# Splitting the transpose of a pair's last row tile in an attention and MoE kernel

## The chip, the cores and the metric

The kernel runs on one core of a Trainium2 chip. The metric is the device time of one execution in microseconds (us); lower is better. The engines are named as in the profile: PE is TensorE, DVE is VectorE, ACT is ScalarE, POOL is GpSimd, and SP is SyncE, which here only issues DMAs.

## What is computed

Attention with a learned position bias, and behind it a feed-forward layer with two weight matrices:

```
B, H, S, D = 4, 8, 576, 64
scores = q @ k.T / sqrt(D) + bias        # bias[h,i,j] from log1p(|i-j|) / log1p(i) through a small MLP
attn   = exp(scores - max) / (sum + 1e-9)
x      = (attn @ v), reshaped to [B*S, H*D] = [2304, 512]
h      = x @ w_in                        # 512 -> 2048
g      = h * clip(h + 3, 0, 6) / 6
out    = g @ w_out                       # 2048 -> 512
```

## The kernel before, in words

**Units.** Two heads make a pair; a batch has four pairs. The 576 query rows of a batch are cut in two parts: part 0 has rows 0 to 255, part 1 rows 256 to 575 (320 rows). A unit is one batch, one pair, one part. All 16 units of part 0 come first, then the 16 units of part 1, batch by batch. The change touches the units of part 1 alone.

**Tiles.** A unit of part 1 has five row tiles of 128 rows (`ORDER`, numbers 4 to 8): rows 256 to 383 of the first head and of the second, rows 384 to 511 of the first and of the second, and a last tile (number 8) with the 64 remaining rows 512 to 575 of both heads, the first head's in partitions 0 to 63 and the second head's in 64 to 127. The tiles of all units stand in one list, and `front(n)` issues work for several of them at once: the maximum of tile n, the scores of tile n+1, the normalization of tile n-1 (`hl`, high part by ACT, L129), the low part of tile n-2 (DVE, L146), the transpose of tile n-3 (`soft_turn`, L648), the product with V of the unit whose last tile is n-5 (`pv_step`, L719) and the low part of x (`x_low`) of the unit whose last tile is n-6. `back(n)` issues `x_high` (ACT, L733) of the unit whose last tile is n-5, and the exponential of tile n (L583).

**Transposes.** The attention rows `hl` are 128 x 1152 in fp16: the high part in columns 0 to 575 and the low part in 576 to 1151. A DMA transpose on SP's queue turns one tile into a 128 x 9 x 128 piece of `at`, at the column `COLS[t]`. In a unit of part 1 `at` has 640 columns, the first head's 320 tokens in columns 0 to 319 and the second head's in 320 to 639.

**x.** The product with V, `pv_ps`, lies in one PSUM bank: the first head in partitions 0 to 63 and the second in 64 to 127, with the columns in the order of `at`. Since the last tile is transposed as one piece to columns 256 to 383, the second head's tokens begin with their last 64. `XPARTS` puts them right: ACT writes the high part of x with three instructions (64 rows x 320, x 64 and x 256 columns), and DVE the low part with three more of the same shapes. The profile calls both L146 (DVE) and L733 (ACT), with `x` as output.

**Banks.** From the stretch that matters here on, `pv_ps` shares four PSUM banks (`w_bank`) with the feed-forward layer's `h_ps` (L794) and `o_ps` (L817). Banks are taken in turn, so the fourth bank taken after a `pv_ps` is that same bank, and PE waits there until DVE's x has read it. The scores `s_ps` (L560) take two other tiles of PSUM in turn, free when DVE's L572 has read them. An `h_ps` bank is free when DVE's L777 (`t`) has read it.

**Order.** PE's instructions keep the order of the program from tile 37 on, and SP's from tile 45 on. DVE, ACT and POOL are ordered by the framework's scheduler.

Of the kernel before, what the change touches and what calls it, by code (L numbers as in the profile page):

```python
# [14 lines left out]
AF = mybir.ActivationFunctionType  # L15
# [20 lines left out]
def attention_moe_kernel(  # L36
# [17 lines left out]
    nc = tc.nc  # L54
# [61 lines left out]
    pscale = {}  # L116
# [28 lines left out]
    def low_part(out, full, scale, high):  # L145
        nc.vector.scalar_tensor_tensor(  # L146
            out=out, in0=full, scalar=scale, in1=high, op0=ALU.mult, op1=ALU.subtract
        )
# [249 lines left out]
    QW = (256, 320)  # L398
# [106 lines left out]
        return out, src  # L505

    ORDER = [(0, 0), (0, 1), (1, 0), (1, 1), (2, 0), (2, 1), (3, 0), (3, 1), (4, 0)]
    COLS = [0, 256, 128, 384, 0, 384, 128, 512, 256]
    UT = (range(4), range(4, 9))
    units = [(b, p, u) for u in range(2) for b in range(B) for p in range(PAIRS)]  # L510
    tiles = [(0, p, t) for ts in ((0, 1), (2, 3)) for p in range(2) for t in ts]
# [10 lines left out]
    a_t = {}  # L522
    at_t = {}
# [87 lines left out]
    def direct(b, p, t):  # L611
        return b < cfg["fb"] and t < 4

    def unit_tile(n):
        b, p, t = tiles[n]
        u = int(t >= 4)
        if (b, p, u) not in at_t:
            if direct(b, p, t):
                at = at_p.tile([128, 5, 512], F32, tag=f"at{p % 2}", name="atf")
            else:  # L620
                at = at_p.tile([128, 9, 2 * QW[u]], F16, tag=f"at{p % 2}", name="at")
            at_t[b, p, u] = at
        return at_t[b, p, u][:, :, COLS[t]:COLS[t] + 128]

    def soft_low(n):
        if direct(*tiles[n]):
            bt, sm = a_t.pop(n)
            tp = s_bank("t_ps").rearrange("p a b -> p (a b)")
            for c in range(5):
                j = 128 * c if c < 4 else 448  # L630
                nc.tensor.transpose(tp[:, 128 * c:128 * c + 128], bt[:, j:j + 128], eye_sb)  # L631
            src = tp[:, 0:640].rearrange("p (c i) -> p c i", c=5)
            if pick("tv", n) == "A":
                nc.scalar.activation(out=unit_tile(n), in_=src, func=AF.Copy)  # L634
            else:
                nc.vector.tensor_copy(out=unit_tile(n), in_=src)
            return
        bt, sm, hl = a_t[n]
        r = sm[:, 3:4]
        if hl_mode(n) in "RS":  # L640
            nc.gpsimd.tensor_sub(out=hl[:, S:], in0=bt, in1=hl[:, 0:S])
        else:
            low_part(hl[:, S:], bt, r, hl[:, 0:S])
        a_t[n] = hl

    def soft_turn(n):
        if not direct(*tiles[n]):
            nc.sync.dma_start_transpose(out=unit_tile(n), in_=a_t.pop(n))  # L648

    XPARTS = [  # L650
        [(slice(0, 128), 0, 256, 0)],
        [
            (slice(0, 64), 0, 320, 0),
            (slice(64, 128), 0, 64, 256),
            (slice(64, 128), 64, 320, 0),
        ],
    ]

    def x_tile(b, u):
        if (b, u) not in x_t:  # L660
            x_t[b, u] = x_p.tile([128, 2, KC, QW[u]], F16, tag="x", name="x")
        return x_t[b, u]
# [27 lines left out]
    def x_first(b, p):  # L690
        ps = pv_t.pop((b, p, 0))
        n = 256
        x = x_tile(b, 0)
        xr = hl_p.tile([128, 2, n], F32, tag="hl", name="xr")
        xs, rb = xr[:, 0], xr[:, 1]
        nc.scalar.activation(
            out=rb, in_=ps[:, 1, 0:n], func=AF.Copy,
            scale=pscale["x1"][:, p:p + 1] if b else pscale["v0"][1],
        )
        if cfg["xp"]:  # L700
            nc.scalar.activation(out=xs, in_=ps[:, 0, 0:n], func=AF.Copy)
            nc.gpsimd.tensor_mul(out=xs, in0=xs, in1=rb)
        else:
            nc.vector.tensor_mul(out=xs, in0=ps[:, 0, 0:n], in1=rb)
        xh = x[:, 0, p]
        nc.scalar.activation(out=xh, in_=xs, func=AF.Copy)
        nc.gpsimd.tensor_sub(out=x[:, 1, p], in0=xs, in1=xh)
# [19 lines left out]
    def x_high(b, p, u):  # L727
        if direct(b, p, 4 * u):
            return x_first(b, p)
        ps = pv_t[b, p, u]  # L730
        x = x_tile(b, u)
        for rows, lo, hi, tok in XPARTS[u]:
            nc.scalar.activation(  # L733
                out=x[rows, 0, p, tok:tok + hi - lo], in_=ps[rows, lo:hi], func=AF.Copy,
                scale=pscale["x"][rows, p:p + 1],
            )

    def x_low(b, p, u):
        if direct(b, p, 4 * u):
            return  # L740
        ps = pv_t.pop((b, p, u))
        x = x_tile(b, u)
        for rows, lo, hi, tok in XPARTS[u]:
            low_part(
                x[rows, 1, p, tok:tok + hi - lo], ps[rows, lo:hi],
                pscale["x"][rows, p:p + 1], x[rows, 0, p, tok:tok + hi - lo],
            )

    def ffn(b, u):
        x = x_t.pop((b, u))  # L750
# [235 lines left out]
    def front(n):  # L986
# [13 lines left out]
        if unit_at(n - 6):  # L1000
            x_low(*unit_at(n - 6))
# [8 lines left out]
        if at(n - 3):  # L1010
            soft_turn(n - 3)
# [12 lines left out]
    def back(n):  # L1024
        if unit_at(n - 5):
            x_high(*unit_at(n - 5))
        if at(n):
            soft_exp(n)
# [60 lines left out]
    for cs in (slice(512, LT), slice(0, 512)):  # L1089
        nc.vector.tensor_scalar(  # L1090
            out=T[:, cs], in0=T[:, cs], scalar1=w1_sb, scalar2=None, op0=ALU.mult
# [13 lines left out]
    for c, pat in enumerate(pats):  # L1105
        for k in range(4):
            if pat[k]:
                rows = slice(32 * k, 32 * k + 32)
# [111 lines left out]
    for n in range(-1, NT + 7):  # L1220
# [19 lines left out]
        if done is not None and done != (0, 0):  # L1240
            b, u = done
# [76 lines left out]
```

## Time and profile before

| what | value |
|---|---|
| time before, median of 3 runs (lowest, highest) | 681.77 us (680.17, 683.64) |
| the profiled execution's own time | 680.92 us |
| its span, from the first to the last instruction | 679.1 us |
| PE busy | 631.2 us, 93% of the span |
| ACT busy | 519.8 us, 77% |
| DVE busy | 478.9 us, 71% |
| POOL busy | 210.6 us, 31% |
| mean granted PE clock | 0.987 of full speed |

Busy shares are averages over the whole span. Most of PE's idle time lies in the first 240 us, in which the weights and the bias tables are prepared; the units of part 1 are worked on from about 340 to 610 us. The profiled execution's time and its span differ by 1.8 us, which lie before the first and after the last instruction.

### The profile page before, as it was taken

How to read it: one execution, taken by the hardware profiler on the slowest of the kernel's cores; microseconds unless marked ns; L12 is line 12 of the kernel's file. 1: busy time of each engine (PE TensorE's matmuls, PEld its weight loads, DVE VectorE, ACT ScalarE, POOL GpSimd, SP SyncE). 2: the span in 40 equal slices, each digit the busy share in tenths (PEclk: the TensorE clock that was granted, in tenths of full speed). 3: DMA queues.
4: the chain of work that ended last, by engine and by line, in shares of the span. 5: the costliest groups of instructions: out<-in, count | busy, mean ns of one | idle time of the engine just before them, and what ended most of it. 6: DMA issues, size and time to landing. Idle time of an engine off the chain costs nothing. (4 is left out here: it accounts for less than half of the span.)

```text
span 679.1 us, 14803 instructions
## 1 busy us (share of the span) xinstructions
PE 631.2 (93%) x5424; PEld 449.8 (66%) x5424; DVE 478.9 (71%) x1150; ACT 519.8 (77%) x1032; POOL 210.6 (31%) x267
## 2 busy tenths in 40 slices
PE   7677889787998999999999999999999999999997
PEld 2224546555676767688887786767776777777775
DVE  7889977999737887777688777777777768811310
ACT  7986877887939997998699878987799779922620
POOL 1111115855102441154134413541244313310420
PEclk9997999997999999999999999999999999999999
DMA  8899768571768979979999899979977796420000
GB/s 295 297 339 339 296 246 317 184 271 57 192 182 208 236 191 283 217 217 203 280 278 232 175 202 195 190 148 181 206 178 150 166 197 126 98 60 20 1 11 29
DMA packets 176136, 130.56 MB, mean 192 GB/s; under 512 B 137792, under 2 KB 145216, under 8 KB 175040
## 3 DMA queue, kind: packets, MB, share of 16 engines
q1 hardware_dynamic: 166272, 114.14, 67.5%
q10 hardware_dynamic: 9792, 15.49, 7.1%
q8 instruction: 42, 0.69, 0.4%
q14 instruction: 30, 0.25, 0.1%
HBM read 77.54 MB, written 15.49 MB: 137 GB/s over the span
## 5 line engine op out<-in xcount | busy, mean ns | idle before, releaser
L794 PE MATMUL h_ps<-x,wi 128*128 128x256 f16 (+1 forms) x1536 | 199.7, 287 | 8.3 <-DVE t L777 4.0
L817 PE MATMUL o_ps<-g,wo 128*128 128x256 f16 (+1 forms) x1536 | 195.8, 286 | 0.3 <-DVE t L777 0.3
L794 PEld LDWEIGHTS <-wi 128*128 128x128 f16 x1536 | 147.2, 98 | 56.5 <-issue 14.4
L817 PEld LDWEIGHTS <-wo 128*128 128x128 f16 x1536 | 147.0, 98 | 47.0 <-issue 10.0
L773 POOL TENSOR_TENSOR g<-t,g 128x256 f16<-128x256 f32 (+1 forms) x128 | 101.6, 805 | 165.1 <-ACT g L771 155.4
L583 ACT ACTIVATE bt<-bt,sm 128x576 f32<-128x576 f32 x144 | 110.6, 769 | 43.6 <-DVE sm L572 41.2
L146 DVE SCALAR_TENSOR_TENSOR hl<-bt,sm,hl 128x576 f16<-128x576 f32 x112 | 93.9, 854 | 25.1 <-ACT hl L129 22.4
L419 POOL TENSOR_TENSOR qkl<-st,qkh 128x576 fp32r<-128x576 f32 (+2 forms) x48 | 56.4, 1196 | 98.3 <-ACT qkh L412 98.2
L129 ACT ACTIVATE hl<-bt,sm 128x576 f16<-128x576 f32 x112 | 83.9, 768 | 2.8 <-ACT bt L583 1.4
L777 DVE SCALAR_TENSOR_TENSOR t<-t,t,h_ps 128x320 f32<-128x320 f32 (+1 forms) x112 | 56.4, 515 | 37.0 <-ACT t L784 35.3
L572 DVE CUSTOM_DVE_ANT_0 bt<-s_ps,bt 128x576 f32<-128x576 f32 x88 | 64.7, 750 | 12.2 <-PE s_ps L560 5.7
L784 ACT ACTIVATE t<-h_ps,t,hr 128x320 f32<-128x320 f32 (+1 forms) x112 | 64.5, 588 | 4.4 <-PE h_ps L794 3.3
L771 ACT ACTIVATE g<-t 128x256 f16<-128x256 f32 (+1 forms) x128 | 55.0, 440 | 15.5 <-DVE t L777 14.8
L827 ACT ACTIVATE ot<-o_ps,os 128x256 f32<-128x256 f32 (+1 forms) x32 | 15.9, 496 | 52.7 <-PE o_ps L817 52.6
L591 DVE TENSOR_SCALAR sm<-sm 128x1 f32<-128x1 f32 x112 | 16.9, 151 | 42.9 <-ACT bt L583 42.7
L869 DVE TENSOR_SCALAR z_e<-T,nbp 128x576 f32<-128x576 f32 (+17 forms) x69 | 36.0, 568 | 4.3 <-PE b_ps L890 4.2
L929 ACT ACTIVATE bo<-b_ps,cv_sb,isc 128x576 f32<-128x576 f32 (+36 forms) x60 | 35.8, 636 | 2.5 <-PE b_ps L890 2.5
L146 DVE SCALAR_TENSOR_TENSOR x<-pv_ps,xr,x 64x320 f16<-64x320 f32 (+3 forms) x56 | 23.6, 445 | 18.1 <-ACT x L733 17.0
L873 ACT ACTIVATE z_e<-T,bp 128x576 f32<-128x576 f32 (+17 forms) x43 | 28.9, 694 | 9.7 <-PE b_ps L890 4.3
L631 PE MATMUL t_ps<-eye_sb,bt 128*128 128x128 f32 x160 | 26.3, 299 | 10.6 <-DVE sm L572 5.7
L631 PEld LDWEIGHTS t_ps<-eye_sb,bt 128*128 128x128 f32 x160 | 18.8, 150 | 20.9 <-ACT atf L634 7.8
L719 PE MATMUL pv_ps<-at,vh 128*64 128x320 f16 (+1 forms) x432 | 32.0, 293 | 0.3 <-DVE t L777 0.3
(127 smaller groups left out, 860.4 us busy)
## 6 DMA issues: line engine op xcount, KB each, us to landing
bt<-bias SPq DMA_DIRECT2D x36, 576.0 KB, 5.0
w<-in_w_in_dram SPq DMA_DIRECT2D x8, 1024.0 KB, 7.2
vs<-in_vp_dram SPq DMA_DIRECT2D x24, 320.0 KB, 4.4
st<-in_qk_dram SPq DMA_DIRECT2D x16, 448.0 KB, 4.6
bias<-bo ACTq DMA_DIRECT2D x20, 295.5 KB, 4.5
wo<-in_w_out_dram SPq DMA_DIRECT2D x5, 1024.0 KB, 5.9
bias<-bo ACTq DMA_DIRECT2D x16, 288.0 KB, 6.3
bt<-bias SPq DMA_DIRECT2D x32, 144.0 KB, 3.2
```

What stands on the lines that cost most here:

```text
L129: nc.scalar.activation(out=out, in_=full, func=AF.Copy, scale=scale)
L146: nc.vector.scalar_tensor_tensor(out=out, in0=full, scalar=scale, in1=high, op0=ALU.mult, op1=ALU.subtract)
L419: nc.gpsimd.tensor_sub(out=lo[:, c:c + w], in0=t[:, c:c + w], in1=hi[:, c:c + w].bitcast(F32))
L572: nc.vector.tensor_tensor_reduce(out=halves(bt), in0=ps, in1=halves(src), op0=ALU.add, op1=ALU.min, scale=-0.125, scalar=3.0e38, accum_out ...
L583: nc.scalar.activation(out=bt, in_=bt, func=AF.Exp, scale=-1.0, bias=sm[:, 0:1], accum_out=total)
L631: nc.tensor.transpose(tp[:, 128 * c:128 * c + 128], bt[:, j:j + 128], eye_sb)
L771: nc.scalar.activation(out=g[:, 0], in_=uu, func=AF.Copy)
L773: e.tensor_sub(out=g[:, 1], in0=uu, in1=g[:, 0])
L777: nc.vector.scalar_tensor_tensor(out=t_t[f], in0=t_t[f], scalar=cols(f)[2], in1=h_t.pop(f)[:, 0:n], op0=ALU.min, op1=ALU.mult,)
L784: nc.scalar.activation(out=t_t[f], in_=h_t[f][:, 0:n], func=AF.Relu, scale=cols(f)[0], bias=cols(f)[1],)
L794: nc.tensor.matmul(out=h_t[f][:, 0:n], lhsT=wi[:, a, c, f * 128:(f + 1) * 128], rhs=x[:, e, c], start=(k == 0), stop=(k == 3 * KC - 1),)
L817: nc.tensor.matmul(out=ops[:, 0:n], lhsT=wo[:, a, f, e * 128:(e + 1) * 128], rhs=g_t[f][:, r], start=(f == 0 and a == 0 and r == 0), stop= ...
```

## The change

Tile 8 is transposed by two DMAs of 64 rows: the first head's half goes to columns 256 to 319 of `at` and the second head's to columns 576 to 639. The second head's other two tiles move from columns 384 and 512 to 320 and 448. Both heads then have the same token order, and x takes one ACT and one DVE instruction of 128 rows x 320 columns.

```diff
-    COLS = [0, 256, 128, 384, 0, 384, 128, 512, 256]
+    COLS = [0, 256, 128, 384, 0, 320, 128, 448, 256]
...
     def soft_turn(n):
-        if not direct(*tiles[n]):
-            nc.sync.dma_start_transpose(out=unit_tile(n), in_=a_t.pop(n))
...
+        hl = a_t.pop(n)
+        if tiles[n][2] < 8:
+            nc.sync.dma_start_transpose(out=unit_tile(n), in_=hl)
+            return
+        at = whole_unit(n)
+        for s in range(2):
+            c = 256 + QW[1] * s
+            nc.sync.dma_start_transpose(out=at[:, :, c:c + 64], in_=hl[64 * s:64 * s + 64])
...
     def x_high(b, p, u):
-        for rows, lo, hi, tok in XPARTS[u]:
-            nc.scalar.activation(
-                out=x[rows, 0, p, tok:tok + hi - lo], in_=ps[rows, lo:hi], func=AF.Copy,
-                scale=pscale["x"][rows, p:p + 1],
-            )
+        nc.scalar.activation(
+            out=x[:, 0, p], in_=ps[:, 0:QW[u]], func=AF.Copy, scale=pscale["x"][:, p:p + 1]
+        )
...
     def x_low(b, p, u):
-        for rows, lo, hi, tok in XPARTS[u]:
-            low_part(
-                x[rows, 1, p, tok:tok + hi - lo], ps[rows, lo:hi],
-                pscale["x"][rows, p:p + 1], x[rows, 0, p, tok:tok + hi - lo],
-            )
+        low_part(x[:, 1, p], ps[:, 0:QW[u]], pscale["x"][:, p:p + 1], x[:, 0, p])
```

The order of PE's instructions is the same in both programs. On SP every transpose of a tile 8 becomes two. On ACT and DVE the three x instructions of each of the 16 units become one, and around the second and third of these units the scheduler also orders other work differently.

On DVE, in the second unit of part 1, the rows before run from `vl` (the low part of V) to the next two row tiles' maxima (ISA, L572, of which the second is left out); `hl` is the low part of a row tile, and `t` the feed-forward layer's L777:

```order
L146 SCALAR_TENSOR_TENSOR vl<-vs,s_v_567,vh 128x640
L591 TENSOR_SCALAR sm<-sm 128x1
L595 RECIPROCAL sm<-sm 128x1
L146 SCALAR_TENSOR_TENSOR x<-pv_ps,xr,x 64x320
L146 SCALAR_TENSOR_TENSOR x<-pv_ps,xr,x 64x64
L146 SCALAR_TENSOR_TENSOR x<-pv_ps,xr,x 64x256
L146 SCALAR_TENSOR_TENSOR hl<-bt,sm,hl 128x576
L777 SCALAR_TENSOR_TENSOR t<-t,t_1740,h_ps 128x256
L146 SCALAR_TENSOR_TENSOR hl<-bt,sm,hl 128x576
L572 ISA bt,sm<-s_ps,k_4753 128x576
```

The same place of the changed program (its line 774 is line 777 of before):

```order
L591 TENSOR_SCALAR sm<-sm 128x1
L595 RECIPROCAL sm<-sm 128x1
L146 SCALAR_TENSOR_TENSOR vl<-vs,s_v_567,vh 128x640
L146 SCALAR_TENSOR_TENSOR x<-pv_ps,xr,x 128x320
L146 SCALAR_TENSOR_TENSOR hl<-bt,sm,hl 128x576 x2
L774 SCALAR_TENSOR_TENSOR t<-t,t_1740,h_ps 128x256 x3
L572 ISA bt,sm<-s_ps,k_4751 128x576
```

Here x is one instruction directly behind `vl`, and the first `t`, which stood between the two `hl`, stands behind both.

On SP, in a unit in the middle of part 1, the rows before run from the load of a last tile's bias (`bt`, 64x576 x2) to the two copies of `vh`; the second of the two transposes in the fourth row is that of a tile 8:

```order
L648 DMA_TRANSPOSE at<-hl 128x9x128
L498 DMA bt<-bias_101 64x576 x2
L450 DMA vs<-in_vp_dram 128x640
L648 DMA_TRANSPOSE at<-hl 128x9x128 x2
L464 DMA vh<-vh 64x512
L465 DMA vh<-vh 64x640
```

The same place of the changed program:

```order
L655 DMA_TRANSPOSE at<-hl 128x9x128
L498 DMA bt<-bias_101 64x576 x2
L450 DMA vs<-in_vp_dram 128x640
L655 DMA_TRANSPOSE at<-hl 128x9x128
L660 DMA_TRANSPOSE at<-hl 128x9x64 x2
L464 DMA vh<-vh 64x512
L465 DMA vh<-vh 64x640
```

One DMA more stands ahead of the copies of `vh`, and nothing else has moved.

## Rows read from the trace of the kernel before

**Rows 1.** The head of the page: the span and the number of instructions.

```profile
span 679.1 us, 14803 instructions
```

**Rows 2.** Windows of part 1's time: length, each engine's busy time, PE clock, DMA.

```profile
340.00:420.00 80.00, 76.39 (x740) 62.86 (x739) 62.77 (x163) 68.72 (x151) 29.59 (x44) 1.00 1.04 222
420.00:600.00 180.00, 178.20 (x1518) 129.55 (x1516) 134.51 (x332) 150.72 (x312) 62.93 (x88) 1.00 0.80 161
```

**Rows 3.** PE's timeline, 340 to 600 us: all rows with idle time (start, length, idle).

```profile
357.92 4.10 PE L794 MATMUL h_ps<-x,wi 128*128 128x256 f16 x36 [0.80 <-DVE x L146]
...
374.07 1.48 PE L794 MATMUL h_ps<-x,wi 128*128 128x256 f16 x12 [0.59 <-DVE x L146]
375.84 2.78 PE L817 MATMUL o_ps<-g,wo 128*128 128x256 f16 x24 [0.28 <-DVE t L777]
...
398.60 0.53 PE L560 MATMUL s_ps<-qkh 64*128 64x288 f32 x3 [0.73 <-DVE sm L572]
...
415.35 0.53 PE L560 MATMUL s_ps<-qkh 64*128 64x288 f32 x3 [1.21 <-DVE sm L572]
...
443.33 3.43 PE L794 MATMUL h_ps<-x,wi 128*128 128x320 f16 x24 [0.86 <-DVE x L146]
...
514.96 5.06 PE L794 MATMUL h_ps<-x,wi 128*128 128x320 f16 x36 [0.94 <-DVE x L146]
```

**Rows 4.** Groups by shape that write x: busy us, mean ns, idle before.

```profile
L146 DVE SCALAR_TENSOR_TENSOR x<-pv_ps,xr,x 64x320 f16<-64x320 f32 x16 | 8.7, 542 | 17.9 <-ACT x L733 17.0
L146 DVE SCALAR_TENSOR_TENSOR x<-pv_ps,xr,x 64x256 f16<-64x256 f32 x16 | 7.8, 487 | 0.0
...
L146 DVE SCALAR_TENSOR_TENSOR x<-pv_ps,xr,x 128x256 f16<-128x256 f32 x8 | 3.8, 476 | 0.0
...
L733 ACT ACTIVATE x<-pv_ps,xr 64x320 f16<-64x320 f32 x16 | 8.2, 509 | 3.1 <-PE pv_ps L719 3.1
```

**Rows 5.** DVE's timeline ahead of PE's first and fourth wait for x.

```profile
355.52 1.18 DVE L146 SCALAR_TENSOR_TENSOR hl<-bt,sm,hl 128x576 f16<-128x576 f32 x1 [0.24 <-DMA at<-hl]
356.62 1.25 DVE L146 SCALAR_TENSOR_TENSOR x<-pv_ps,xr,x 64x320 f16<-64x320 f32 x3
...
442.03 1.25 DVE L146 SCALAR_TENSOR_TENSOR x<-pv_ps,xr,x 64x320 f16<-64x320 f32 x3
```

**Rows 6.** The timeline ahead of PE's second and third wait.

```profile
371.54 1.19 ACT L733 ACTIVATE x<-pv_ps,xr 64x320 f16<-64x320 f32 x3
...
372.76 1.25 DVE L146 SCALAR_TENSOR_TENSOR x<-pv_ps,xr,x 64x320 f16<-64x320 f32 x3 [0.70 <-ACT x L733]
...
375.30 0.48 DVE L777 SCALAR_TENSOR_TENSOR t<-t,t,h_ps 128x256 f32<-128x256 f32 x1
```

**Rows 7.** The timeline ahead of PE's first wait for DVE's L572.

```profile
389.83 1.44 ACT L129 ACTIVATE hl<-bt,sm 128x576 f16<-128x576 f32 x2
389.84 1.25 DVE L146 SCALAR_TENSOR_TENSOR x<-pv_ps,xr,x 64x320 f16<-64x320 f32 x3 [0.70 <-ACT x L733]
...
391.13 1.55 DVE L146 SCALAR_TENSOR_TENSOR hl<-bt,sm,hl 128x576 f16<-128x576 f32 x2
```

**Rows 8.** The same ahead of PE's second wait for L572.

```profile
406.40 1.25 DVE L146 SCALAR_TENSOR_TENSOR x<-pv_ps,xr,x 64x320 f16<-64x320 f32 x3
```

**Rows 9.** The transposes of part 1's time by their line: ns min/median/max; landing.

```profile
L648 SPq DMA_TRANSPOSE at<-hl x75: 1242/1305/2611, 342.0 to 597.5; - x75
...
DMA to landing us min/median/max: 3.2/3.9/6.8
```

**Rows 10.** SP's queue around one tile 8, and the chain's row of its product with V.

```profile
436.85 1.82 SPq L648 DMA_TRANSPOSE at<-hl  x1
439.90 0.49 SPq L464 DMA_DIRECT2D vh<-vh  x1
...
453.46 2.02 PE pv_ps L719 x28
```

**Rows 11.** A window around the last transpose, with no other transfer (columns as in Rows 2).

```profile
598.00:601.00 3.00, 3.00 (x24) 2.16 (x23) 1.24 (x3) 0.05 (x1) 0.08 (x1) 1.00 0.51 98
```

More of the change, by code (lines that the diff above doesn't have):

```diff
@@ L612, in direct, with whole_unit @@
         return b < cfg["fb"] and t < 4
-    def unit_tile(n):
+    def whole_unit(n):
         b, p, t = tiles[n]
@@ L622, in unit_tile @@
             at_t[b, p, u] = at
-        return at_t[b, p, u][:, :, COLS[t]:COLS[t] + 128]
+        return at_t[b, p, u]
+    def unit_tile(n):
+        c = COLS[tiles[n][2]]
+        return whole_unit(n)[:, :, c:c + 128]
     def soft_low(n):
@@ L646, in soft_turn @@
     def soft_turn(n):
-        if not direct(*tiles[n]):
-            nc.sync.dma_start_transpose(out=unit_tile(n), in_=a_t.pop(n))
[L650 to L657, printed above, removed]
+        if direct(*tiles[n]):
+            return
+        hl = a_t.pop(n)
+        if tiles[n][2] < 8:
+            nc.sync.dma_start_transpose(out=unit_tile(n), in_=hl)
+            return
+        at = whole_unit(n)
+        for s in range(2):
+            c = 256 + QW[1] * s
+            nc.sync.dma_start_transpose(out=at[:, :, c:c + 64], in_=hl[64 * s:64 * s + 64])
     def x_tile(b, u):
```

## The prediction

> **What bounds the kernel now.** I read the busy shares by window first. From 340 to 420 us PE is busy 76.39 of 80 us, and from 420 to 600 us 178.20 of 180 us, at the full granted clock [rows 2]. So PE bounds the part of the program that the change touches, and all that can be won there without touching PE's own work is its idle time: 3.61 + 1.80 = 5.41 us of a span of 679.1 us [rows 1, 2]. Behind 600 us PE runs without a gap to the end, so a microsecond won earlier arrives at the end whole.
>
> PE's timeline shows where the 5.41 us lie: in seven places, and their idle times add up to just that sum, 0.80 + 0.59 + 0.28 + 0.73 + 1.21 + 0.86 + 0.94 [rows 3]. I call them A to G in this order. A, B, F and G, 3.19 us, end when DVE has finished x: the `h_ps` that waits is the fourth bank after a `pv_ps` and takes its PSUM bank. C ends with DVE's L777, which frees an `h_ps` bank. D and E end with DVE's L572, which frees a tile of scores. The reader should see that the change shortens the very work that four of the seven places wait for, and that this is under one per cent of the time at most.
>
> **The price of x.** Instructions cost by columns, not by rows: a DVE instruction of 128 rows x 256 columns takes 476 ns and one of 64 x 256 takes 487 [rows 4]. So the new instruction of 128 x 320 should take what 64 x 320 takes, 0.54 us on DVE and 0.51 us on ACT [rows 4]. Today the three take 1.25 us on DVE and 1.19 on ACT [rows 5, 6]. Each unit saves 0.71 us on DVE and 0.68 on ACT, 16 units 11 us on each. That would be the gain if DVE or ACT bounded the kernel; as it is, only what shortens the seven waits counts.
>
> **Wait by wait.** In A, x starts on DVE when the `hl` ahead of it ends, at 356.7 us, and ends at 357.87; PE goes on at 357.92 [rows 3, 5]. The changed program keeps `hl` ahead of x here, so x ends 0.71 us earlier: 0.71 of 0.80 is saved. F is the same case (x from 442.03 to 443.28, PE from 443.33 [rows 3, 5]), 0.71 of 0.86. G has the same rows 72 us later, 0.71 of 0.94.
>
> In B, DVE's x waits for ACT's, which ends at 372.73 [rows 6]. Both get shorter, 0.68 + 0.71 = 1.39 us, more than the wait: all 0.59 is saved.
>
> In C, the order in front of L777 changes. Before, x ended at 374.01, one `hl` followed, `t` took 375.30 to 375.78 and PE went on at 375.84 [rows 3, 6]. Now `t` stands behind two `hl`, of some 0.8 us each (two take 1.55 [rows 7]). x ends about 372.6, the two `hl` about 374.2 to 374.6, `t` about 374.7 to 375.1. The bank is free 0.7 to 1.1 us earlier than before; but PE, which has won 0.71 + 0.59 and would save C's 0.28 too, arrives at 374.26. So the wait becomes 0.5 to 0.85 us in place of 0.28. I book a loss of 0.40, between the bounds of a loss of 0.57 and a gain of 0.28 (if `t` is early enough).
>
> In D and E, PE waits for a chain through DVE and ACT. Ahead of D, x waits for ACT's x, and two `hl` follow, the first of which also needs an ACT `hl` that starts right behind ACT's x [rows 7]. With x at its new length the ACT `hl` starts 0.68 us earlier and DVE is free 1.39 us earlier; the DVE `hl` (now 391.13) can start when the first ACT `hl` ends, at 389.15 + 0.72 = 389.9, so the chain comes 1.2 us earlier. Ahead of E, x (406.40) starts when DVE is free [rows 8], so only its 0.71 counts. PE reaches D 0.90 us earlier (A, B and C together). If nothing else in the chain moves, D's wait becomes 0.73 + 0.90 - 1.2 = 0.43 and E's 1.21 + (0.90 + 0.30) - (1.2 + 0.71) = 0.50, which saves 0.30 + 0.71 = 1.0 us. If the chain also follows PE's earlier start, both waits go, 1.94 us. I take the lower end, 1.0, as the rows show no reason that the scheduler's new order upstream is any faster.
>
> **The price of the second transpose.** No row shows a transpose of 64 rows. Its issue on SP costs between half of today's 1.3 us (if it goes by rows) and all of it [rows 9], so a tile 8 costs SP between nothing and 1.3 us more. I take 0.3. Behind a tile 8, SP's next DMA, L464, starts 1.23 us after the transpose has been issued (436.85 + 1.82 = 438.67, next 439.90 [rows 10]), because it waits for ACT's `vh`; that gap hides nearly all of the upper bound. Landing has more room: issued at 436.85, landed at most 6.8 us later, and the product that reads it starts at 453.46 [rows 9, 10], which leaves 9.8 us. Even a second transpose that waits for the first to land and takes the median 3.9 us more is in time. So this costs PE nothing, unless the DMA engines themselves become the limit. A lone transpose fills them for 0.51 x 3 = 1.53 us [rows 11]; two halves cost between that and twice as much. I take no more than now, as the bytes are the same.
>
> **The sum.** 0.71 (A) + 0.59 (B) - 0.40 (C) + 1.0 (D and E) + 0.71 (F) + 0.71 (G) = 3.3 us. The profiled execution took 680.92 us, so it would take 677.6. The median of the runs is 0.85 us above the profiled one, so I forecast 681.77 - 3.3 = **678.4 us** for the median, just at 0.5% less (3.4 us), which is about the least that a measurement of this kernel tells from no change, as its three runs alone spread over that much.
>
> **The rivals.**
>
> *The gain is taken back (0 to 2.4 us).* ACT's and DVE's new order around the second and third unit of part 1 could make waits C, D and E grow by what A and B saved: PE arrives earlier at scores and banks that are no earlier. C above shows how, and DVE's and ACT's share of 340 to 420 us, 62.8 and 68.7 of 80 us [rows 2], leaves little room there. Then only F and G count, 1.4 us: 680.4 us. Against it: each unit also gives ACT 0.68 us, and the chain should follow.
>
> *All seven waits go (over 4.4 us).* If ACT, relieved of 0.68 us in every unit, runs ahead of PE throughout, up to 5.4 us are won: 676.4 us. For it: ACT is busy 86% of the time from 340 to 420 us [rows 2], where five of the seven waits stand. Against it: D and E are chains of dependent work, not of load.
>
> *Slower: the DMA engines become the limit.* Between 340 and 420 us their mean busy share is 1.04 [rows 2]; nothing in the rows says that they could take more there. If a transpose of 64 rows fills them as long as one of 128, each of the five units in this stretch adds 1.53 us [rows 11], 7.7 us in all, and loads and transposes come later by as much. With F and G saved, that is 681.77 + 7.7 - 1.4 = 688.1 us. The Trainium skill (DMA: Bandwidth & Descriptors, Rules for kernel authors) speaks against this very edit: it says not to split a transfer into disjoint partition halves, since they serialize on the same engines. By that rule alone the halves win nothing and, at worst, cost what this rival says; no run here shows it yet. It decides from the point at which the extra time in the queue exceeds the 9.8 us of room, or reaches the loads of bias ahead of L572. Against it: not one of the seven waits ends with a DMA [rows 3], and the same bytes should need the same time.
>
> **Chances and range.** The forecast (2.4 to 4.4 us won) 0.47, the gain taken back 0.27, all waits gone 0.16, slower 0.10. Faster by over 0.5% is the 0.16 of the second rival and a good half of the forecast's case, 0.43 in all; slower is 0.10; the rest, 0.47, lies within 0.5%. The range for 8 in 10 goes from 676.2 us (all 5.4 us won) to 682.2 us (nothing won, and the spread of a median); it leaves out most of the slower rival. The forecast's own range is 677.4 to 679.4 us.
>
> **What would show it.** In the changed profile x should be 16 instructions of 128x320 on DVE near 0.54 us and 16 on ACT near 0.51. PE's idle time from 340 to 600 us should fall from 5.4 to about 2.1 us, with A, F and G under 0.25 us each and B gone; C should be the one that grows. SP's transposes of 64 rows should take 0.65 to 1.3 us, and no PE wait should end with a DMA. The forecast is wrong if PE idles elsewhere (in `pv_ps`, for `at`), if DVE waits for bias loads, or if the halves fill the DMA engines as long as the whole.

## The result and the profile after

The changed kernel takes 675.41 us (median of 8 runs, 674.25 to 677.73). The kernel before takes 681.08 us in 8 runs beside it (679.37 to 683.64). The ratio is 0.9919, with a 95% interval from 0.9896 to 0.9943. The forecast was 678.4 us with a range of 676.2 to 682.2, so the time fell 3.0 us below the forecast and 0.8 us below the range.

The head of the changed kernel's page answers [rows 1], and the windows answer [rows 2]; the columns are the same.

```profile
span 673.4 us, 14770 instructions
```

```profile
340.00:420.00 80.00, 79.10 (x765) 64.80 (x764) 62.53 (x159) 69.15 (x148) 29.32 (x45) 1.00 1.07 224
420.00:600.00 180.00, 180.00 (x1535) 131.04 (x1532) 121.49 (x303) 138.04 (x283) 62.58 (x86) 1.00 0.81 160
```

PE's idle time from 340 to 600 us has gone from 5.41 to 0.90 us. From 420 us on PE does not wait at all. From 340 to 420 us DVE and ACT are about as busy as before, while PE gets through more of the program in that time (765 matmuls in place of 740); behind 420 us DVE is busy 13.0 us less and ACT 12.7 us less.

PE's timeline has two rows with idle time left. The first is C, the only one of the seven waits of [rows 3] that is still there. The second stands ahead of a score product where there was no wait before.

```profile
374.06 2.78 PE L814 MATMUL o_ps<-g,wo 128*128 128x256 f16 x24 [0.44 <-DVE t L774]
...
380.98 0.53 PE L560 MATMUL s_ps<-qkh 64*128 64x288 f32 x3 [0.38 <-DVE sm L572]
```

The groups that write x, by shape, answer [rows 4] (busy us, mean ns, idle before).

```profile
L146 DVE SCALAR_TENSOR_TENSOR x<-pv_ps,xr,x 128x320 f16<-128x320 f32 x16 | 8.7, 542 | 14.7 <-ACT x L735 14.6
L735 ACT ACTIVATE x<-pv_ps,xr 128x320 f16<-128x320 f32 x16 | 8.1, 509 | 3.2 <-PE pv_ps L722 3.1
```

The instruction of 128 x 320 costs what 64 x 320 cost, to the nanosecond: 542 and 509 ns.

The transposes of 64 rows answer [rows 9] (ns min/median/max of the issue on SP).

```profile
L660 SPq DMA_TRANSPOSE at<-hl x32: 1198/1269/1997, 337.7 to 592.9; - x32
...
DMA to landing us min/median/max: 2.8/3.9/6.7
```

A half costs SP 1.27 us, nearly the 1.31 us of a whole one [rows 9], and lands after the same median of 3.9 us.

**Where the time came from.** PE executes the same 5424 matmuls in every kernel of this study, and from 350 us on in the same order, but for a few products that run side by side; only line numbers differ. So one can subtract, for each matmul, its start in one trace from its start in the other, and see at which place the difference changes. The table lists these changes in us (positive is time won against the profiled execution of before) from 350 us on: at the places A to G, at the new wait, and in the rest up to the end. The labels other than `after` are those of the experiments below.

```
                      A      B      C    new      D      E      F      G   rest     sum
after              0.72   0.63  -0.16  -0.77   1.13   1.60   0.91   1.02   0.06   5.14
after_again        0.70   0.64  -0.18  -0.76   1.10   1.59   0.92   1.02   0.06   5.09
e9_three_dmas      0.69   0.63  -0.17  -0.77   1.13   1.60   0.91   1.02   0.07   5.11
e11_four_late      0.70   0.63  -0.16  -0.76   1.12   1.60   0.91   1.02  -0.30   4.75
e4_four_dmas       0.70   0.64  -0.18  -0.75   1.13  -2.58   0.92   1.02  -0.30   0.59
e1_three_x        -0.01   0.01   0.01   0.00  -0.00   0.00  -0.01  -0.00   0.00  -0.01
e2_act_one        -0.00  -0.89   0.44  -0.01   1.12   0.91   0.54   0.63  -0.01   2.72
e3_dve_one         0.69  -1.51   0.44   0.01   1.13   1.34   0.72   0.98  -0.21   3.60
e5_batch0          0.70   0.63  -0.17  -0.78   1.13   1.60   0.09  -0.01   0.00   3.19
e6_batch123       -0.00  -0.00  -0.00   0.01  -0.02   0.00   0.92   1.02   0.06   2.00
e12_two_units0    -0.01   0.00   0.00   0.00   1.13   1.60   0.08  -0.00  -0.01   2.81
e7_two_units      -0.01   0.01   0.01  -0.01   0.00   0.00   0.75   0.76  -0.45   1.08
e8_filler          0.52  -1.87   0.44   0.01   1.10   1.08   0.93   1.02  -0.49   2.74
```

The change wins 5.14 us there. The rest of the 5.7 us between the two spans, 0.59 us, lies ahead of 350 us. It is there at 300 us already, ahead of the first split transpose at 337.7 us, so it is none of the change's doing: executions differ by that and more in that stretch.

D and E show why idle time is not the whole price of a wait. These are PE's rows at D, of before and of the changed kernel; the row of before is the one ahead of 398.60 in [rows 3].

```profile
397.48 0.40 PE L560 MATMUL s_ps<-qkh 64*128 64x288 f32 x1
```

```profile
396.47 0.53 PE L560 MATMUL s_ps<-qkh 64*128 64x288 f32 x4
```

The score products of two row tiles with the same rows, one tile of each head, come in pairs, one product for each head on 64 rows of the array, and the two of a pair start 3 ns apart in the trace. (A tile 8 is not among them: its products take all 128 rows.) Before, the first of the pair had its tile and started at 397.48, and the second had to wait until 398.60: it was 1.13 us late. The view counts 0.73 us of it as idle, since PE is "busy" with the lone first product for the other 0.40. Without the wait all four run in 0.53 us. So D cost 1.13 and E 1.60 us, 0.8 us more together than their idle rows say. The Trainium skill (TensorE: Matmul & The Clock Gate, Why this matters for your kernels) says that products with few rows in distinct row groups run concurrently, with starts at most 4 ns apart; the trace agrees, with 3 ns.

### The profile page after: what moved, and what is told of

Same layout as the page of the kernel before. It is cut to its first block, busy times and chain, and to the rows that moved or that the text cites. A ratio compares the mean times of both kernels' runs of the same rounds, so it can differ in the third digit from the quotient of the medians.

```text
span 673.4 us, 14770 instructions
## 1 busy us (share of the span) xinstructions
PE 634.7 (94%) x5424; PEld 452.7 (67%) x5424; DVE 463.7 (69%) x1118; ACT 506.8 (75%) x1000; POOL 209.2 (31%) x267
## 5 line engine op out<-in xcount | busy, mean ns | idle before, releaser
L572 DVE CUSTOM_DVE_ANT_0 bt<-s_ps,bt 128x576 f32<-128x576 f32 x88 | 64.7, 750 | 13.9 <-PE s_ps L560 7.5
L572 DVE CUSTOM_DVE_ANT_0 bt<-s_ps,k 128x576 f32<-128x576 f32 x40 | 28.7, 752 | 7.0 <-PE s_ps L560 6.9
L259 POOL TENSOR_SCALAR w<-w 128x1024 f32<-128x1024 f32 x8 | 10.2, 1278 | 66.3 <-ACT wo L258 47.6
```

The lines of the kernel that those rows point to most:

```text
L572: nc.vector.tensor_tensor_reduce(out=halves(bt), in0=ps, in1=halves(src), op0=ALU.add, op1=ALU.min, scale=-0.125, scalar=3.0e38, accum_out ...
```

## Experiments

All ratios are against runs of the kernel before on the same chip, with 95% intervals. Each kernel is described by its difference from the changed kernel.

**The split alone, and each engine's part alone.** The theory was that the shorter x on both engines is what PE sees, through banks and score tiles that are free earlier, and that the split of the transpose costs nothing. Its rivals were that the split itself gives or takes time, and that the relief of one engine alone is enough.

`e1_three_x` keeps the two DMAs and gives x its three instructions back, on both engines:

```diff
+    def XP(b, u):
+        top, low = slice(0, 64), slice(64, 128)
+        if u == 0:
+            return [(slice(0, 128), slice(0, QW[u]))]
+        return [(top, slice(0, 320)), (low, slice(0, 64)), (low, slice(64, 320))]
...
-        nc.scalar.activation(
-            out=x[:, 0, p], in_=ps[:, 0:QW[u]], func=AF.Copy, scale=pscale["x"][:, p:p + 1]
-        )
+        for rows, cs in XP(b, u):
+            nc.scalar.activation(
+                out=x[rows, 0, p, cs], in_=ps[rows, cs], func=AF.Copy,
+                scale=pscale["x"][rows, p:p + 1],
+            )
```

with the same loop around `low_part`. `e2_act_one` has that loop on DVE alone, `e3_dve_one` on ACT alone.

> The changed kernel with its two transposes of 64 rows, but x written by three ACT and three DVE instructions of the shapes of before (64x320, 64x64, 64x256); the engines' order is that of before on PE, DVE, ACT and POOL. Theory (the gain is x's shorter time on DVE and ACT): all of the gain is gone, ratio to before 1.000 within 0.003, PE's idle time from 340 to 600 us about 5.4 us again in the same seven places. Rival (the split of the transpose helps by itself): some 5 us stay won, ratio 0.992. Rival (the split costs something that the shorter x hid): ratio over 1.003, with PE waits that end with a transpose.

Measured: 680.65 us, ratio 1.0004 (0.9986 to 1.0022). All seven waits are back, and the table has 0.01 us at most at each place. The split is free here, and no more than free: it wins nothing without the shorter x.

> As the changed kernel, but DVE writes the low part of x by three instructions; ACT keeps the one. Theory: waits A, F and G of the rows ahead of the prediction are set by DVE and stay; B goes, since ACT's x ends 0.68 us earlier; D and E lose some of their 1.94 us: 1 to 2.5 us won, ratio 0.9965 to 0.9985, PE idle 340 to 600 us 3 to 4.5 us. Rival (the gain is the relief of ACT, the busier engine): 4 us or more stay won, ratio 0.993 to 0.994. Rival (the new order around the second and third unit): the time follows whichever order the scheduler takes, not the engine.

Measured: 678.05 us, ratio 0.9964 (0.9947 to 0.9981), 2.72 us in the table. A stays, as expected, but F and G were expected to stay too and shrink to 0.3 us: ACT's short x alone wins 0.54 and 0.63 us there. One wait at B grows:

```profile
372.88 1.47 PE L800 MATMUL h_ps<-x,wi 128*128 128x256 f16 x12 [1.39 <-DVE t L783]
```

> As the changed kernel, but ACT writes the high part of x by three instructions; DVE keeps the one. Theory: A, F and G save 0.7 to 0.9 us each, B its 0.6, D and E some 0.7 each: 3 to 4.5 us won, ratio 0.9935 to 0.9955, PE idle 340 to 600 us 1 to 2.5 us. Rival (the gain is the relief of ACT): under 1.5 us won, ratio over 0.998.

Measured: 677.79 us, ratio 0.9950 (0.9931 to 0.9968), 3.60 us in the table. One wait is left, also at B:

```profile
371.31 1.47 PE L799 MATMUL h_ps<-x,wi 128*128 128x256 f16 x12 [2.00 <-DVE t L782]
```

In both, the scheduler orders DVE's `t` around the second unit in a third way, and PE waits there for it, longer than in either kernel (-0.89 and -1.51 in the table). Outside B and C, where that order acts, one engine's short x alone gives 3.2 and 4.7 us and both give 4.7. D goes in each of them, but PE comes to D 0.5 and 0.4 us later than before, so what one engine's part does at D and E is not shown. F and G lie far behind that place: there ACT's part alone wins 1.17 us, DVE's 1.70 and both 1.93. So neither part is without effect, and the two do not add.

**Where the gain is made.** `e5_batch0` has the short x in the first batch's units alone, `e6_batch123` in the other three batches' alone. Both use the loop of `e1_three_x` on both engines, under a condition:

```diff
-        if u == 0:
+        if u == 0 or b == 0:          # e5_batch0; b > 0 in e6_batch123
             return [(slice(0, 128), slice(0, QW[u]))]
```

> x takes one instruction of 320 columns in the first batch's units alone; the other three batches use three instructions. If each of PE's waits is shortened by the work taken out in its own batch, A to E go as in the changed kernel (net some 3.2 us by its trace) and F and G stay at 0.86 and 0.94: a ratio near 0.995. If the lead that the first batch gains is kept and used up later, F and G shrink too, by up to 0.4 us each, and the ratio is near 0.994. If F and G carry the gain, it is 1.000.

> The complement: one instruction of 320 columns in the last three batches, three in the first. A to E stay (0.80, 0.59, 0.28, 0.73, 1.21). By the price of x alone F and G shrink by 0.71 us each, 1.4 us in all (ratio 0.998); if the lead builds up over a batch's units, both vanish, 1.8 to 1.9 us (ratio 0.997). The gains of this kernel and of the one with the first batch alone should add up to that of the change (5.1 us from PE's first wait on).

Measured: 677.19 us, ratio 0.9953 (0.9936 to 0.9969), and 678.71 us, ratio 0.9970 (0.9951 to 0.9989). The table has 3.19 and 2.00 us, which add up to 5.19 against 5.14 for both. The first batch wins all of A to E, and 0.09 of F; the others win F and G whole. So the lead does not carry from one batch to the next, and the first of the three readings that was written down for `e5_batch0` holds. PE's rows at F and G in it:

```profile
439.93 3.43 PE L802 MATMUL h_ps<-x,wi 128*128 128x320 f16 x24 [0.75 <-DVE x L146]
...
511.57 5.06 PE L802 MATMUL h_ps<-x,wi 128*128 128x320 f16 x36 [0.95 <-DVE x L146]
```

`e7_two_units` and `e12_two_units0` go down to single units: the short x in the two units right ahead of F and G, and in the two ahead of D and E. DVE's and ACT's order is then nearly that of before.

```diff
+        if u == 0 or (b, p) in ((1, 1), (2, 1)):    # e7_two_units; ((0, 2), (0, 3)) in e12_two_units0
```

> One instruction of 320 columns in two units alone, the ones whose x stands right before the waits F and G. By the price of x alone F and G fall by 0.71 us each, to 0.15 and 0.23; if they vanish here too, the price of x was too low; if they vanish only in the kernel with all units of these batches, the rest of the gain is a lead that the units before build up. Ratio 0.998.

Measured: 679.74 us, ratio 0.9983 (0.9967 to 1.0000). F and G become 0.75 and 0.76 us shorter, a little over the price of x. F is gone, and of G this is left:

```profile
515.10 5.06 PE L802 MATMUL h_ps<-x,wi 128*128 128x320 f16 x36 [0.19 <-DVE x L146]
```

The remaining 0.16 and 0.26 us of the change at these places come from the other units of the same batches. The 0.45 us in the column "rest" are lost at one place, a pair of score products at 524.16 us, of which the second waits for DVE's L572.

> One instruction of 320 columns in two units alone, the ones whose x lies ahead of the waits D and E. Each of these waits costs 0.73 and 1.21 us of idle time and, as the offsets between the runs show, another 0.4 us in which the first of a pair of score products runs alone. If the two short x are enough, both waits go: 2.7 us (ratio 0.996). By the sum of the prediction, in which nothing but x itself moves, some 1.2 us of D's chain and 1.9 of E's are won, D goes (1.1 us) and about half of E stays: 1.9 us (ratio 0.997). If D and E went in the changed kernel because the units before had already moved DVE's chain ahead, both stay in large part: under 1.5 us (ratio 0.998). A, B and C stay as before.

Measured: 677.44 us, ratio 0.9954 (0.9938 to 0.9970), 2.81 us in the table. D and E go whole, 1.13 and 1.60 us, and A, B and C stay as they were. PE's rows, of the timeline around C and D:

```profile
373.80 2.78 PE L825 MATMUL o_ps<-g,wo 128*128 128x256 f16 x24 [0.27 <-DVE t L785]
...
395.44 0.53 PE L560 MATMUL s_ps<-qkh 64*128 64x288 f32 x4
```

So two of the sixteen short x bring more than half of the gain, and no lead from the units ahead of them is needed for it. The reading by the prediction's sum, in which half of E stays, did not come: it moved the chain ahead of E by too little.

**Engine time or earlier release?** `e8_filler` is the changed kernel with two instructions more behind each x on DVE and on ACT, of the sizes that x has lost and with results that nothing reads.

```diff
+        if u:
+            for n in (64, 256):
+                nc.scalar.activation(
+                    out=fill[0][0:64, 0:n], in_=x[0:64, 0, p, 0:n], func=AF.Copy, scale=1.0
+                )
...
+        if u:
+            for n in (64, 256):
+                nc.vector.scalar_tensor_tensor(
+                    out=fill[1][64:128, 0:n], in0=x[64:128, 1, p, 0:n], scalar=1.0,
+                    in1=x[64:128, 1, p, 0:n], op0=ALU.mult, op1=ALU.subtract,
+                )
```

> The changed kernel with two idle copies of x's old sizes behind each x on DVE and on ACT (64x64 and 64x256, to a scratch tile), so that the engines' busy time is that of before or a little more, while x itself is done as early as in the changed kernel. If the gain is the earlier x alone, A, B, F and G stay won (some 3 us) and D and E, where DVE's and ACT's load counts, return in part: ratio near 0.996. If the gain is the load taken off the engines, most of it is gone: ratio near 1.000.

Measured: 679.31 us, ratio 0.9977 (0.9961 to 0.9994); the table has 2.74 us for its profiled execution, just above what the interval allows. F and G stay won (0.93 and 1.02), A in part (0.52). That speaks for the earlier release at these three places. At B a wait of 2.37 us appears in this order too (`<-DVE t`), so PE arrives late at D and E, and their 1.10 and 1.08 us say nothing on load. For D and E this run is inconclusive.

**How much splitting SP bears.** `e4_four_dmas` cuts tile 8 in four DMAs of 32 rows, `e9_three_dmas` in three (64, 32 and 32 rows), and `e11_four_late` in four from the second batch on and in two in the first.

```diff
-        for s in range(2):
-            c = 256 + QW[1] * s
-            nc.sync.dma_start_transpose(out=at[:, :, c:c + 64], in_=hl[64 * s:64 * s + 64])
+        for k in range(4):                # e4_four_dmas
+            c = 256 + QW[1] * (k // 2) + 32 * (k % 2)
+            nc.sync.dma_start_transpose(out=at[:, :, c:c + 32], in_=hl[32 * k:32 * k + 32])
```

> As the changed kernel, but tile 8 is transposed by four DMAs of 32 rows. Theory (the extra DMAs lie in SP's idle time and in the 9.8 us before the product with V): the time of the changed kernel, ratio to before 0.992 within 0.003, PE idle 340 to 600 us about 1 us, no PE wait that ends with a DMA, SP 2.5 us busier in each of the 16 units if issue does not go by rows. Rival (the second DMA already costs something, hidden under the gain): two more cost at least 1 us in all, ratio 0.9935 or more, and PE waits ahead of pv_ps.

Measured: 682.02 us, ratio 1.0003 (0.9979 to 1.0027). That was a miss: the whole gain is gone in the median, though two of the twelve executions, with 676.33 and 677.35 us, are as fast as the changed kernel; only one execution, of 682.56 us, was traced. The table puts nearly all of the loss in one place, E, with 2.58 us lost in place of 1.60 won. PE's row there, then ACT's timeline ahead of it with its output DMA, and the answer on L655, the transposes of 128 rows whose issue was under way from 404.9 to 413.5 us (ns of the issue, who waited for them, landing):

```profile
416.99 0.52 PE L560 MATMUL s_ps<-qkh 64*128 64x288 f32 x3 [2.17 <-DVE sm L572]
```

```profile
410.11 0.76 ACT L129 ACTIVATE hl<-bt,sm 128x576 f16<-128x576 f32 x1
413.21 0.35 ACTq L826 DMA_DIRECT2D out_dram<-ot  x1
413.67 0.62 ACT L781 ACTIVATE t<-h_ps,t,hr 128x320 f32<-128x320 f32 x1 [2.79 <-DMA at<-hl]
```

```profile
L655 SPq DMA_TRANSPOSE at<-hl x2: 1316/1454/1592, 404.0 to 407.3; - x2
...
  ACT t L781: 2.8, 1
...
DMA to landing us min/median/max: 4.6/5.2/5.9
```

The reader should see that PE waits for DVE, and DVE for ACT, while ACT stood 2.79 us in front of a DMA of its own. That DMA only stores `ot`, which was ready at 409.45. The records give it the same semaphore as a transpose that SP issued at 407.27 and that landed 5.9 us later, and it waits for that landing. In the changed kernel the same pair exists, but there the transpose is issued at 398.54 and the output DMA at 407.11, and nothing waits. The margin between the issue of the transpose and the end of `ot` has shrunk from 8.1 to 2.2 us, because SP's queue runs late. Adding up the rows of SP's timeline from 340 to 420 us, its issues take 59.5 of 80 us in the kernel before, 72.7 in the changed one, and 75.5 with three DMAs as with four: at that share the queue has hardly any room left, and each further issue comes later. An issue of 32 rows costs 1.25 us, nearly as much as one of 128. Of the 2.58 us lost at E, 0.96 us are the wait itself, which is that much longer than E was before; the other 1.6 us are lost right behind it, where PE ran at a lower granted clock for a while (windows of 5 us, columns as in [rows 2]):

```profile
415.00:420.00 5.00, 3.01 (x31) 2.25 (x33) 3.55 (x10) 4.96 (x11) 3.90 (x6) 0.84 0.63 124
420.00:425.00 5.00, 5.00 (x37) 3.20 (x34) 4.59 (x12) 4.53 (x10) 1.88 (x3) 0.81 1.06 227
```

> The last row tile by three DMAs (64, 32 and 32 rows); DVE's and ACT's instructions in the changed kernel's order. If more DMAs cost only by a stall of ACT's output DMA behind a transpose that is in flight, as the kernel with four showed it, the time is the changed kernel's (ratio 0.992) unless such a stall shows in ACT's idle time; if each DMA costs by itself, the gain is about half lost (ratio 0.996).

Measured: 674.28 us, ratio 0.9896 (0.9873 to 0.9918), 5.11 us in the table: the changed kernel again, though its SP has no gap of over 0.3 us from 385 to 416 us either. The same transpose and the same output DMA share a semaphore here too. The transpose is issued at 404.86 and lands 4.3 us later, `ot` ends at 409.54, 4.7 us behind the issue, and ACT does not wait. So the margin falls from 8.1 to 4.7 and 2.2 us with two, three and four DMAs, and only the last is shorter than the landing. A third DMA per unit costs nothing by itself.

> Four DMAs of 32 rows in the last three batches, two of 64 rows in the first. If the kernel with four everywhere lost because SP's queue, which has no gap between 385 and 416 us there, ran late by the issues of the first batch and one output DMA on ACT then waited 2.8 us for a late transpose, this one keeps the whole gain: ratio near 0.992, no wait of ACT for a transpose, PE without a wait of 2 us near 417 us. If every further DMA costs by itself, it loses three quarters of the gain: ratio near 0.998.

Measured: 676.51 us, ratio 0.9935 (0.9916 to 0.9954), 4.75 us in the table. No ACT row waits for a transpose and E is won (1.60). The 0.30 us that it has less lie at one place, the pair of score products of which `e7_two_units` and `e8_filler` lose 0.45 and 0.49 us with two DMAs, so they are not shown to be a price of the further DMAs. So four DMAs are all but harmless in twelve of the sixteen units, and the loss of `e4_four_dmas` comes from the first batch, where SP has no room left. This fits the late semaphore; that it is the only path from the first batch's issues to the loss was not tried.

**Once more.** The changed kernel itself, unaltered.

> The changed kernel once more, unaltered: its ratio should fall in 0.990 to 0.994, its trace from PE's first wait on should show again 5.1 us less than before, and what differs ahead of that wait, where both kernels run the same program, is what executions differ by (1 to 3 us).

Measured: 677.08 us, ratio 0.9933 (0.9910 to 0.9957), and 5.09 us in the table, the same at each place to 0.03 us. Ahead of 350 us its trace is 3.2 us later than that of before, where the first one was 0.6 us earlier, with the same program. The medians of both sets of runs, 675.41 and 677.08 us, contain such differences; the table does not. The second median lies inside the forecast's range, the first below it.

## Why the prediction was wrong, step by step

The working assumed that an idle row of PE is the price of its wait, took for each wait the gain that x alone gives with all else in place, and chose the lower bound where a chain was involved. The mechanism was right at A, B, C, F and G, where the terms came out right or too small. Ahead of E it was wrong, and one step that the order should have told was missing.

- **The price of x**: right, 542 and 509 ns for a forecast of 0.54 and 0.51 us.
- **A, B**: booked 0.71 and 0.59, measured 0.72 and 0.63. Right.
- **C**: booked -0.40, measured -0.16. C grew, as the working said, from 0.28 to 0.44 us, through the two `hl` ahead of `t`. DVE's timeline of the changed kernel answers [rows 6]:

```profile
370.69 0.89 DVE L146 SCALAR_TENSOR_TENSOR vl<-vs,s_v,vh 128x640 f16<-128x640 f32 x1 [0.37 <-ACT vh L129]
371.49 0.55 DVE L146 SCALAR_TENSOR_TENSOR x<-pv_ps,xr,x 128x320 f16<-128x320 f32 x1
372.07 1.55 DVE L146 SCALAR_TENSOR_TENSOR hl<-bt,sm,hl 128x576 f16<-128x576 f32 x2
373.54 1.26 DVE L774 SCALAR_TENSOR_TENSOR t<-t,t,h_ps 128x256 f32<-128x256 f32 x3
```

  This trace is 0.59 us ahead of that of before, so x ends at 372.6 and PE arrives at 374.2 by the times of before, both as forecast. The two `hl` end at the early end of what was booked, and the first `t` is done at 374.6, not at 374.7 to 375.1.

- **The step that was missing**: a new wait at 380.98 us, which takes back 0.77 us (0.38 of idle time and the 0.40 of a lone first product). DVE's rows ahead of that score tile, of the changed kernel and of before:

```profile
378.28 0.82 DVE L146 SCALAR_TENSOR_TENSOR hl<-bt,sm,hl 128x576 f16<-128x576 f32 x1 [0.31 <-ACT hl L129]
379.25 0.99 DVE L146 SCALAR_TENSOR_TENSOR hl<-bt,sm,hl 128x576 f16<-128x576 f32 x1 [0.15 <-ACT hl L129]
380.17 0.74 DVE L572 CUSTOM_DVE_ANT_0 bt<-s_ps,bt 128x576 f32<-128x576 f32 x1
```

```profile
379.67 0.76 DVE L572 CUSTOM_DVE_ANT_0 bt<-s_ps,bt 128x576 f32<-128x576 f32 x1
...
380.92 2.03 DVE L146 SCALAR_TENSOR_TENSOR hl<-bt,sm,hl 128x576 f16<-128x576 f32 x2 [0.49 <-ACT hl L129]
```

  The scheduler has moved L572 behind two `hl` that wait for ACT. Before, the tile was free at 380.4 and PE came at 381.97; now it is free at 380.9 and PE wants it at 380.2. This is the rival "the gain is taken back", in one place: with C it eats 0.93 of the 1.35 us that A and B win.

- **D and E, the step that failed**: the working let the chain come 1.2 us earlier ahead of D and 1.2 + 0.71 = 1.9 us ahead of E ("only its 0.71 counts"), and then "I take the lower end, 1.0", out of 1.0 to 1.94. Measured are 1.13 and 1.60, 2.73 us, or 1.96 us with the new wait set against it. Two things were wrong. The price of the waits was read from their idle rows, 1.94 in place of 2.73. And the gain of the chain was booked too small. In `e12_two_units0` the short x of these two units alone, with PE no earlier, ends both waits whole. DVE's L572 that ends D and the one that ends E, of before and of that kernel, whose trace is 2.04 us ahead by then (C's row, 373.80 for 375.84):

```profile
397.79 0.75 DVE L572 CUSTOM_DVE_ANT_0 bt<-s_ps,bt 128x576 f32<-128x576 f32 x1
...
414.54 0.75 DVE L572 CUSTOM_DVE_ANT_0 bt<-s_ps,bt 128x576 f32<-128x576 f32 x1
```

```profile
394.20 0.75 DVE L572 CUSTOM_DVE_ANT_0 bt<-s_ps,bt 128x576 f32<-128x576 f32 x1
...
409.62 0.75 DVE L572 CUSTOM_DVE_ANT_0 bt<-s_ps,bt 128x576 f32<-128x576 f32 x1
```

  With the 2.04 us taken off, they start 1.55 and 2.88 us earlier, where 1.2 and 1.9 were booked. At E the working had read that x (406.40 [rows 8]) starts when DVE is free, so that ACT's short x counts for nothing there. The rows beside it, of before and then of `e12_two_units0`, say otherwise:

```profile
405.18 1.19 ACT L733 ACTIVATE x<-pv_ps,xr 64x320 f16<-64x320 f32 x3
...
405.45 0.81 DVE L146 SCALAR_TENSOR_TENSOR hl<-bt,sm,hl 128x576 f16<-128x576 f32 x1
...
408.54 0.76 DVE L572 CUSTOM_DVE_ANT_0 bt<-s_ps,k 128x576 f32<-128x576 f32 x1
```

```profile
401.84 0.81 DVE L146 SCALAR_TENSOR_TENSOR hl<-bt,sm,hl 128x576 f16<-128x576 f32 x1
402.57 0.55 DVE L146 SCALAR_TENSOR_TENSOR x<-pv_ps,xr,x 128x320 f16<-128x320 f32 x1
403.03 0.81 DVE L146 SCALAR_TENSOR_TENSOR hl<-bt,sm,hl 128x576 f16<-128x576 f32 x1
403.76 0.75 DVE L572 CUSTOM_DVE_ANT_0 bt<-s_ps,k 128x576 f32<-128x576 f32 x1
```

  Before, DVE was free at 406.26 and ACT's x ended at 406.37: x stood 0.14 us for it, which the view does not mark. From `hl` to L572 DVE takes 3.09 us before and 1.92 us with the short x, 1.17 less in place of 0.71: x starts 0.22 us sooner behind `hl`, and L572 0.95 us sooner behind the start of x, since the instructions also follow a single x more closely. The reason given for the lower end, that no row shows the new order to be faster upstream, was no reason against the price of the two x themselves.

- **F and G**: booked 0.71 each, measured 0.91 and 1.02. `e7_two_units` gives the booked size for x alone (0.75 and 0.76); the rest is what the other units of the batch add, which the sum left out.
- **The second transpose**: at SP's queue a half costs 1.27 us, so a tile 8 costs 1.23 us more, near the upper bound of the forecast, and not 0.3, but PE sees nothing of it (`e1_three_x`). The room of 9.8 us was read for one path, the product with V, and PE never waits there; `e4_four_dmas` loses on a path that the working did not have, the output DMA of ACT. The slower rival, with the DMA engines as the limit, did not come: their share is 1.07 and 0.81, against 1.04 and 0.80 [rows 2]. The Trainium skill (DMA: Bandwidth & Descriptors, Rules for kernel authors) advises against two transfers to disjoint partition halves, since they serialize. Here the halves are those of the source, and each is written to all 128 partitions of `at`, so the rule bears on this edit less squarely than the prediction has it. As far as it goes it is half borne out: the halves win nothing by themselves, ratio 1.0004, and pay for SP's issue twice, but what they save behind the transfer is worth it here.

The terms together: 0.72 + 0.63 - 0.16 - 0.77 + 2.73 + 0.91 + 1.02 + 0.06 = 5.14 us, against 3.3 booked. The outcome falls to the rival "all seven waits go" (over 4.4 us), which had a chance of 0.16. Of the seven, six went. Its reason, an ACT that runs ahead of PE throughout, is not what the runs show: `e5_batch0`, `e6_batch123` and `e12_two_units0` put the gain in the batch, and at D and E in the two units, right ahead of each wait.

The median lies below the range for one reason more: 681.77 less 5.14 is 676.6 us, within the range. The median of three runs that the sum started from was 0.7 us above that of the eight runs beside the changed kernel, 681.08.

Of the signs named, the x groups, the loss of A, B, F and G, the growth of C, SP's issue time and the lack of a PE wait on a DMA came as forecast. The idle time of 2.1 us did not; it was 0.9, and PE idled in one new place, ahead of a score product.

## What to carry to other kernels

A short stall is priced by how late the next instruction starts, not by its idle row: here, where two products on half the rows each run side by side, a wait of the second hides another 0.4 us. Before a row is said to start when its engine is free, its start is set against the end of what it reads on the other engines: a wait of 0.14 us showed no mark and decided a term. Where a chain of dependent work ends in the wait, first take all that shortens the chain, and take the lower bound only if a row names what would hold the chain back. Subtracting the starts of the same PE instruction in two traces finds the place of tenths of a microsecond that the medians of runs, 1 to 3 us apart for the same program, cannot show.

## What the hardware showed that was not expected

- The issue of a DMA transpose costs SP nearly the same for 32, 64 and 128 rows: medians of 1.25, 1.27 and 1.31 us. Splitting is paid in the queue; the median time to landing does not rise (3.4, 3.9 and 3.9 us).
- An output DMA that only stores a result can stop the engine that issues it: ACT stood 2.79 us, because its DMA's semaphore was still that of a transpose in flight.
- The granted clock fell to 0.84 and 0.81 (means of 5 us, between the two levels of 1.2 and 2.4 GHz) behind the wait of 2.17 us in `e4_four_dmas`. In `e3_dve_one` and `e8_filler`, behind waits of 2.00 and 2.37 us, it stayed at 1.00. The runs do not tell what makes the difference.
